# Start and end of a fused attention and gated-MLP block: how the modulation weight and c are read, which banks hold the first queries, and when the last output tiles are finished

## The chip, the cores and the metric

The kernel runs on one core of a Trainium2 chip. The metric is the device time of one execution in microseconds (us). The time before is the median of four runs, and one further execution was taken by the hardware profiler; all durations below come from that one.

## The reference

```python
mod = (silu(c) @ w_mod).reshape(1, 6, 1, 512)      # c: 1x512, w_mod: 512x3072
sa, ca, ga, sb, cb, gb = mod[:, 0..5]
h = layernorm(x) * (1 + ca) + sa                   # x: 1x2048x512
x = x + ga * A(h)      # 32 query heads over 8 cached key/value heads, 2048 keys, 128 wide, then wo
h = layernorm(x) * (1 + cb) + sb
x = x + gb * B(h)      # gelu(h @ w_in) halves z1, z2; layernorm(z2); w_sp @ z2 + b_sp; (z1 * g) @ w_out
```

All tensors are bf16. `A` is softmax attention without a mask: `q = h @ wq`, scores over the cached keys times 128^-0.5, softmax, times the cached values, then `@ wo`. In `B`, `w_sp` is 2048x2048 and mixes the rows.

## The kernel before, in words

The program is written out fully in Python; within each engine the order of instructions is the order of the source, laid out by hand (`manual_schedule`), with a table `at(unit, slot, ...)` that puts side work into slots of the attention loop. Semaphore waits follow from the tiles that an instruction reads and writes. PSUM has eight banks, held by three names: `misc` (two tiles of one bank), `o_ps` (two of one bank) and `s_ps` (two of two banks, by `bank2`). A name's tiles are taken in turn, so that a new tile waits for the one two before it.

**Start, before the attention loop.** ACT's queue reads c (`c_bf`, line 696) with element `4p + j` in partition p, column j. SP's queue reads the first tile of x, the first third of `w_mod` in four parts (`wmod_a`, L699; part kt holds rows `4p + kt`), half of the first keys (`k_nat`, L704), the query weight of the first key head (`wq_g`, L715), the second half of `k_nat`, more of x, and so on. DVE clears a tile `zeros`, and PE runs matmuls on it whose results nobody reads (`warm(n)`, L776). DVE and ACT make `silu(c)` in bf16 (`sc_bf`, L761 to L770). DVE and POOL normalise the first 128 rows of x (`xn1`, L691 to L680). PE makes shift and scale as columns from the four parts (`mod_part`, L868), with pairs of warm matmuls between, turns the normalised rows (L900), and DVE and ACT apply shift and scale while copying them out (`hT`, L828 and L908). Then PE turns four key blocks (`k_turn`, L883) which DVE and ACT copy (L886), 16 matmuls make the first 128 queries of four heads (L921) in the two banks of one `s_ps` tile, and DVE and ACT copy one bank each to `qT` (L929). One more warm matmul, and the loop begins.

**Attention loop.** 128 units of (key head, 128 query rows), eight slots each: PE makes scores (`qk`, L980), ACT takes the exponential (L987), PE multiplies with the values of the unit before (`pv`, L1002), DVE divides, and the output projection of an older unit runs beside it (L1034), as do the query projections (L947). The other two thirds of `w_mod` are read by POOL's queue in unit 2 (L1153) and used from unit 9 on (L792).

**MLP.** The spatial product is made in four chunks of 512 rows. In the last chunk the first 384 columns of each of the seven blocks of `yT` come first; the last 128 columns follow, block by block (L1347, with the bias added by a one-row matmul, L1355), and DVE multiplies them with `z1` (L1363). The output matmuls (L1368) trail by one block. `finish_tile` scales by `gb` (L1380), adds x (L1381) and issues the output DMA on ACT's queue (L1382). In the last chunk it is called for tiles 0, 1, 2 beside blocks f = 1, 3, 5:

```python
        if f % 2 == 1:
            finish_tile(last, f // 2, o2_last[f // 2])
```

**Fallback.** A flag says whether some softmax sum left a safe range; then `general_path` would redo everything. `redo = nc.values_load(flag...)` (L1418) loads it into a register of each of the five engines ahead of the last seven blocks, and `tc.If(redo != 0)` (L1432) is a compare-and-branch on each engine, which here jumps over the whole fallback to the end.

Of the kernel before, what the change touches and what calls it, by code (L numbers as in the profile page):

```python
# [10 lines left out]
BF16 = mybir.dt.bfloat16  # L11
FP32 = mybir.dt.float32
ACT = mybir.ActivationFunctionType
ALU = mybir.AluOpType
AX = mybir.AxisListType
P = 128
# [559 lines left out]
def kernel(  # L576
# [19 lines left out]
    nc = tc.nc  # L596
    _, S, D = A_x.shape
    _, HKV, SK, DH = A_k_cache.shape
    HQ = A_wq.shape[1] // DH
    REP = HQ // HKV  # L600
# [5 lines left out]
    NDT = D // P  # L606
# [3 lines left out]
    CT = 512 // P  # L610
# [8 lines left out]
    out_dram = out[0].rearrange("(t p) d -> p t d", p=P)  # L619
# [3 lines left out]
    HK = SK // 2  # L623
    k_rows = A_k_cache[0, 0, 0:HK].rearrange("(p t) d -> p t d", p=P)
    v_rows = A_v_cache[0, 0, 0:HK].rearrange("(p t) d -> p t d", p=P)
    wmod_dram = w_mod.rearrange("(p dt) n -> p dt n", p=P)
    c_dram = c[0].rearrange("(p j) -> p j", p=P)
    win_dram = B_w_in.rearrange("(dt p) f -> p dt f", p=P)
    wout_dram = B_w_out.rearrange("(ft p) d -> p ft d", p=P)

# [2 lines left out]
    flag = flagp.tile([1, 1], mybir.dt.int32, name="flag")  # L633
# [4 lines left out]
    res = fast.enter_context(tc.tile_pool(name="res", bufs=1))  # L638
# [4 lines left out]
    late = free_b.enter_context(tc.tile_pool(name="late", bufs=2, side="right"))  # L643
    early = free_a.enter_context(tc.tile_pool(name="early", bufs=2))

    x_sb = res.tile([P, NT, D], BF16, name="x_sb")
    ga_rows = res.tile([P, D], FP32, name="ga_rows")
    gb_rows = res.tile([P, D], FP32, name="gb_rows")
# [11 lines left out]
    ident = res.tile([P, P], BF16, name="ident")  # L660
    ones_bf = res.tile([P, P], BF16, name="ones_bf")

    def bank(name):
        return psum.tile([P, 512], FP32, name=name)

    def bank2():
        return psum.tile([P, 1024], FP32, name="s_ps")

    def rstd_of(mv, n, tag):

        ve = stat.tile([P, CT], FP32, name=f"ve_{tag}")
        nc.gpsimd.tensor_scalar(
            out=ve[:, :n], in0=mv[:, :, 1], scalar1=LN_EPS, scalar2=None, op0=ALU.add
        )
        rstd = stat.tile([P, CT], FP32, name=f"rstd_{tag}")
        nc.gpsimd.tensor_tensor(out=rstd[:, :n], in0=ve[:, :n], in1=mhalf[:, :n], op=ALU.pow)
        return rstd

    def normalise(dst, src, mv, rstd):
        nc.vector.tensor_scalar(  # L680
            out=dst,
            in0=src,
            scalar1=mv,
            scalar2=rstd,
            op0=ALU.subtract,
            op1=ALU.mult,
        )

    def ln_stats(mv, j, src):
        st = stat.tile([P, 1, nc.vector.BN_STATS_DIM], FP32, name="bnst")  # L690
        nc.vector.bn_stats(out=st[:, 0, :], in_=src)  # L691
        nc.vector.bn_aggr(out=mv[:, j, :], in_=st[:])


    c_bf = res.tile([P, NDT], BF16, name="c_bf")
    nc.scalar.dma_start(out=c_bf[:], in_=c_dram)
    nc.sync.dma_start(out=x_sb[:, 0, :], in_=x_dram[:, 0, :])
    for kt in range(NDT):
        nc.sync.dma_start(out=wmod_a[:, kt, :], in_=wmod_dram[:, kt, 0 : 2 * D])  # L699
# [53 lines left out]
        nc.sync.dma_start(out=x_sb[:, tiles, :], in_=x_dram[:, tiles, :])  # L753
    load_wo(0, nc.sync)


    zeros = late.tile([P, REP, DH], BF16, name="onorm", bufs=3)
    nc.vector.memset(zeros[:], 0.0)
    nc.vector.memset(ones_bf[:], 1.0)
    c_f = res.tile([P, NDT], FP32, name="c_f")  # L760
    nc.vector.tensor_copy(out=c_f[:], in_=c_bf[:])  # L761
    en = res.tile([P, NDT], FP32, name="en")
    nc.scalar.activation(out=en[:], in_=c_f[:], func=ACT.Exp, scale=-1.0)
    nc.vector.tensor_scalar_add(out=en[:], in0=en[:], scalar1=1.0)
    sig = res.tile([P, NDT], FP32, name="sig")
    nc.vector.reciprocal(out=sig[:], in_=en[:])
    sc = res.tile([P, NDT], FP32, name="sc")
    nc.vector.tensor_tensor(out=sc[:], in0=c_f[:], in1=sig[:], op=ALU.mult)
    sc_bf = res.tile([P, NDT], BF16, name="sc_bf")
    nc.vector.tensor_copy(out=sc_bf[:], in_=sc[:])  # L770

    def warm(n):

        w_ps = bank("o_ps")
        for k in range(n):
            nc.tensor.matmul(  # L776
                w_ps[:].rearrange("p (r d) -> p r d", r=REP),
                lhsT=zeros[:, 0, :],
                rhs=zeros[:],
                start=True,  # L780
                stop=True,
            )
# [26 lines left out]
    def ln1_stats(j0, n):  # L809
        for j in range(j0, j0 + n):  # L810
            ln_stats(mv1, j, x_sb[:, j, :])
        return rstd_of(mv1[:, j0 : j0 + n, :], n, "ln1")

    def ln1_norm(j0, n, rstd):
        xns = []
        for j in range(j0, j0 + n):
            xn = res.tile([P, D], BF16, name="xn1", bufs=4)
            normalise(xn[:], x_sb[:, j, :], mv1[:, j, 0:1], rstd[:, j - j0 : j - j0 + 1])
            xns.append(xn)
        return xns  # L820
# [65 lines left out]
            copy(out=kT0[:, part[0] * P : (part[-1] + 1) * P], in_=k_ps[:, 0 : n * P])  # L886


    xns0 = ln1_norm(0, 1, ln1_stats(0, 1))
    mc_ps = bank("misc")  # L890
    warm(10)
    for kt in range(NDT - 1):
        mod_part(kt, mc_ps)
        warm(2)
    x_ps = []
    for half in range(2):
        x_ps.append(bank(("misc", "o_ps")[half])[:].bitcast(BF16))
        for k in range(2):
            dt = 2 * half + k
            nc.tensor.transpose(  # L900
                x_ps[half][:, k * P : (k + 1) * P], xns0[0][:, dt * P : (dt + 1) * P], ident[:]
            )
# [3 lines left out]
    for k in range(2):  # L906
        ln1_mod(hTs[0][:, k, 0:P], x_ps[0][:, k * P : (k + 1) * P], k)
        nc.scalar.activation(  # L908
            out=hTs[0][:, 2 + k, 0:P],
            in_=x_ps[1][:, k * P : (k + 1) * P],  # L910
            func=ACT.Identity,
            scale=modc[:, NDT + 2 + k : NDT + 3 + k],
# [1 line left out]
        )  # L914
    k_turn((0, 1, 2, 3), (nc.vector.tensor_copy, nc.scalar.copy))
    qTs = {0: early.tile([P, REP, 512], BF16, name="qT")}
    q_ps = bank2()
    for n, dt in enumerate((0, 2, 1, 3)):
        for hh in range(REP):
            c0 = hh // 2 * 512 + hh % 2 * P  # L920
            nc.tensor.matmul(  # L921
                q_ps[:, c0 : c0 + P],
                lhsT=wqs[0][:, dt, hh * DH : (hh + 1) * DH],
                rhs=hTs[0][:, dt, 0:P],
                start=(n == 0 and hh % 2 == 0),
                stop=(n == NDT - 1 and hh % 2 == 1),
            )
    for hf, copy in enumerate((nc.vector.tensor_copy, nc.scalar.copy)):
        copy(  # L929
            out=qTs[0][:, 2 * hf : 2 * hf + 2, 0:P],  # L930
            in_=q_ps[:, hf * 512 : hf * 512 + 2 * P].rearrange("p (h q) -> p h q", h=2),
        )
    warm(1)

    def qproj(b, heads, c0, n):

# [376 lines left out]
    for f in range(NFT):  # L1313
# [6 lines left out]
        out=ok1[:], in0=rall[:], scalar1=1.0 / SAFE, scalar2=None, op0=ALU.is_ge  # L1320
# [8 lines left out]
        out=bad[:], in0=okm[:], scalar1=-1.0, scalar2=1.0, op0=ALU.mult, op1=ALU.add  # L1329
# [37 lines left out]
    def o2_mm(dst, yT, jj, f):  # L1367
        nc.tensor.matmul(  # L1368
            dst,
            lhsT=yT[:, f, jj * P : (jj + 1) * P],  # L1370
            rhs=wout_sb[:, f, :],
            start=(f == 0),
            stop=(f == NFT - 1),
        )

    def finish_tile(t, jj, src):
        j = t * CT + jj
        tmp = mlp.tile([P, D], FP32, name="tmp", bufs=2)
        yout = mlp.tile([P, D], BF16, name="yout", bufs=2)
        nc.vector.tensor_tensor(out=tmp[:], in0=src, in1=gb_rows[:], op=ALU.mult)  # L1380
        nc.vector.tensor_tensor(out=yout[:], in0=tmp[:], in1=x_sb[:, j, :], op=ALU.add)  # L1381
        nc.scalar.dma_start(out=out_dram[:, j, :], in_=yout[:])  # L1382

    yTs = {}

    def o2_tile(t, jj):
        o2 = bank("o_ps")
        for f in range(NFT):
            o2_mm(o2[:], yTs[t], jj, f)
        finish_tile(t, jj, o2[:])  # L1390

    last = NCH - 1
    n_a = 512 - P
# [15 lines left out]
    o2_last = [acc[jj // 2][:, (jj % 2) * 512 : (jj % 2 + 1) * 512] for jj in range(CT)]  # L1409
    yT = yTs[last]  # L1410
    for f in range(NFT):
        spatial(last, yT, f, 0, n_a)
        if f < CT:
            o2_tile(last - 1, f)
        if f > 0:
            for jj in range(CT - 1):
                o2_mm(o2_last[jj], yT, jj, f - 1)
    redo = nc.values_load(flag[0:1, 0:1], min_val=0, max_val=P)  # L1418
    for f in range(NFT):
        spatial(last, yT, f, n_a, P, bias_by_pe=True)  # L1420
        if f == 0:
            for jj in range(CT - 1):
                o2_mm(o2_last[jj], yT, jj, NFT - 1)
        else:
            o2_mm(o2_last[CT - 1], yT, CT - 1, f - 1)
        if f % 2 == 1:
            finish_tile(last, f // 2, o2_last[f // 2])
    o2_mm(o2_last[CT - 1], yT, CT - 1, NFT - 1)
    finish_tile(last, CT - 1, o2_last[CT - 1])
    fast.close()  # L1430

    with tc.If(redo != 0):  # L1432
        general_path(
            tc, A_x, A_k_cache, A_v_cache, A_wq, A_wo, B_x, B_w_in, B_w_sp, B_b_sp, B_w_out,
            c, w_mod, out,
        )
# [30 lines left out]
```

## Time and profile before

| what | value |
|---|---|
| median of 4 runs | 1324.24 us (1323.87 to 1324.52) |
| profiled execution: its time | 1324.25 us |
| profiled execution: span, first to last instruction | 1322.5 us |
| PE busy | 1312.0 us, 99% of the span |
| ACT busy | 1077.6 us, 81% |
| DVE busy | 472.6 us, 36% |
| mean granted TensorE clock | 0.999 |

How to read what follows. "PE" is TensorE's matmuls, "PEld" its weight loads, "DVE" VectorE, "ACT" ScalarE, "POOL" GpSimd, "SP" SyncE; a "q" after the name (SPq, ACTq) stands for the engine's instruction queue, with DMA issues, branches and semaphore waits, which are not counted as busy. A group's row gives the line of the source, the engine, the operation and the tiles (out<-in). A matmul's row is longer than its share of a stream: matmuls are pipelined. In the chain that ended last, each piece has its start, its length and what it was.

### The profile page before, as it was taken

How to read it: one execution, taken by the hardware profiler on the slowest of the kernel's cores; microseconds unless marked ns; L12 is line 12 of the kernel's file. 1: busy time of each engine (PE TensorE's matmuls, PEld its weight loads, DVE VectorE, ACT ScalarE, POOL GpSimd, SP SyncE). 2: the span in 40 equal slices, each digit the busy share in tenths (PEclk: the TensorE clock that was granted, in tenths of full speed). 3: DMA queues.
4: the chain of work that ended last, by engine and by line, in shares of the span. 5: the costliest groups of instructions: out<-in, count | busy, mean ns of one | idle time of the engine just before them, and what ended most of it. 6: DMA issues, size and time to landing. Idle time of an engine off the chain costs nothing.

```text
span 1322.5 us, 27873 instructions
## 1 busy us (share of the span) xinstructions
PE 1312.0 (99%) x12332; PEld 858.3 (65%) x12332; DVE 472.6 (36%) x1166; ACT 1077.6 (81%) x1061; POOL 48.9 (4%) x92
## 2 busy tenths in 40 slices
PE   8999999999999999999999999999999999999998
PEld 5666666666666666666666666666666666644445
DVE  5632222222222222222222222222222566794444
ACT  6898999999999999999999999999999999650000
POOL 1200000000000000000000000000000000020000
PEclk9999999999999999999999999999999999999999
DMA  6451022102111112111110221121101111144300
GB/s 179 128 117 33 13 49 37 37 13 53 25 29 33 34 37 37 29 37 37 33 33 17 53 37 30 21 53 18 34 16 21 25 32 31 33 112 84 69 21 26
DMA packets 148208, 58.12 MB, mean 44 GB/s; under 512 B 138384, under 2 KB 143760, under 8 KB 148080
## 3 DMA queue, kind: packets, MB, share of 16 engines
q1 hardware_dynamic: 141424, 37.78, 14.9%
q0 software_dynamic: 4208, 16.39, 4.2%
q10 hardware_dynamic: 2448, 2.10, 0.5%
q8 instruction: 98, 1.61, 0.5%
q14 instruction: 30, 0.25, 0.1%
HBM read 21.37 MB, written 2.10 MB: 18 GB/s over the span
## 4 chain that ended last, share of the span: by engine, by line
PE 99%; DMA 0%; DVE 0%; SPq 0%; issue 0%; ACT 0%
PE o_ps L1002 35%; PE s_ps L980 33%; PE misc L1034 8%; PE misc L947 8%; PE misc L1347 7%; PE s_ps L1193 2%; PE s_ps L1232 2%; PE o_ps L1368 1%; PE s_ps L1368 1%; DMA wq_g<-in_A_wq_dram 0%; PE misc L1104 0%; SPq L699 0%; DVE tmp L1380 0%; DVE yout L1381 0%; PE s_ps L921 0%; PE misc L1355 0%
## 5 line engine op out<-in xcount | busy, mean ns | idle before, releaser
L987 ACT ACTIVATE pT<-s_ps 128x1024 bf16<-128x1024 f32 x1024 | 1044.3, 1025 | 83.0 <-PE s_ps L980 8.9
L1002 PEld LDWEIGHTS <-pT 128*128 128x128 bf16 x8192 | 548.5, 98 | 241.2
L1002 PE MATMUL o_ps<-v,pT 128*128 128x129 bf16 x8192 | 631.4, 220 | 0.0
L980 PE MATMUL s_ps<-qT,kT 128*128 128x512 bf16 x2048 | 609.0, 379 | 0.7 <-ACT qT L929 0.7
L1013 DVE RECIPROCAL rall<-o_ps 128x2 f32<-128x2 f32 x256 | 43.7, 171 | 744.6 <-PE o_ps L1002 744.4
L980 PEld LDWEIGHTS <-kT 128*128 128x128 bf16 x2048 | 199.4, 98 | 119.2 <-issue 1.4
L1034 PE MATMUL misc<-wo_g,oT 128*128 128x512 bf16 x512 | 194.0, 379 | 0.0
L947 PE MATMUL misc<-hT,wq_g 128*128 128x512 bf16 (+2 forms) x528 | 189.6, 371 | 0.0
L1014 DVE TENSOR_TENSOR onorm<-o_ps,rall 128x256 bf16<-128x256 f32 x256 | 108.6, 424 | 9.0 <-DVE rall L1013 0.3
L1347 PE MATMUL misc<-wsp,z 128*128 128x512 bf16 (+2 forms) x560 | 100.7, 336 | 0.0
L958 DVE CAST qT<-misc 128x512 bf16<-128x512 f32 x127 | 86.2, 680 | 2.3 <-PE misc L947 2.2
L1347 PEld LDWEIGHTS <-z 128*128 128x128 bf16 x560 | 50.6, 98 | 48.5
L1047 DVE TENSOR_TENSOR xacc<-misc,xacc 128x512 f32<-128x512 f32 x112 | 76.1, 680 | 0.0
L947 PEld LDWEIGHTS <-wq_g 128*128 128x128 bf16 x528 | 50.6, 98 | 1.1 <-issue 0.2
L1034 PEld LDWEIGHTS <-oT 128*128 128x128 bf16 x512 | 50.1, 98 | 0.8
L1362 DVE TENSOR_TENSOR gb<-misc,bsp_bc 128x512 bf16<-128x512 f32 (+1 forms) x28 | 18.4, 658 | 59.1 <-PE misc L1347 59.1
L1193 PE MATMUL s_ps<-win_sb,hT 128*128 128x448 bf16 x128 | 27.0, 352 | 0.0
L1203 ACT ACTIVATE z<-s_ps 128x896 bf16<-128x896 f32 x16 | 14.7, 917 | 14.9 <-PE s_ps L1193 14.9
L1232 PE MATMUL s_ps<-hT,win_sb 128*128 128x512 bf16 x112 | 24.5, 379 | 0.0
L1240 ACT ACTIVATE z1T<-s_ps 128x1024 bf16<-128x1024 f32 x14 | 14.3, 1024 | 10.1 <-PE s_ps L1232 9.1
L691 DVE BATCH_NORM_STATS2 bnst<-x_sb 128x6 f32<-128x512 bf16 x32 | 21.9, 683 | 0.5
L715 POOL DMA_DIRECT2D wq_g<-in_A_wq_dram x7 | 5.3, 752 | 420.9 <-PE misc L947 420.9
(86 smaller groups left out, 281.6 us busy)
## 6 DMA issues: line engine op xcount, KB each, us to landing
wq_g<-in_A_wq_dram POOLq DMA_DIRECT2D x7, 512.0 KB, 3.9
v<-in_A_v_cache_dram POOLq DMA_DIRECT2D x7, 512.0 KB, 6.6
wo_g<-in_A_wo_dram POOLq DMA_DIRECT2D x7, 512.0 KB, 4.7
oT<-onorm SPq DMA_TRANSPOSE x128, 2.4
wsp<-in_w_mod_dram POOLq DMA_DIRECT2D x1, 2048.0 KB, 10.5
out_dram<-yout ACTq DMA_DIRECT2D x16, 128.0 KB, 1.7
win_sb<-in_B_w_in_dram POOLq DMA_DIRECT2D x1, 1792.0 KB, 7.7
x_sb<-in_A_x_dram SPq DMA_DIRECT2D x3, 512.0 KB, 5.6
```

What stands on the lines that cost most here:

```text
L947: nc.tensor.matmul(ps[0][:, o0 : o0 + n], lhsT=wqs[g][:, dt, hh * DH : (hh + 1) * DH], rhs=hTs[ch][:, dt, c0 : c0 + n], start=(dt == 0), s ...
L958: nc.vector.tensor_copy(out=dst, in_=src)
L980: nc.tensor.matmul(s_ps[:, h * 512 : (h + 1) * 512].rearrange("p (r q) -> p r q", r=REP), lhsT=groups[g]["kT"][:, kt * P : (kt + 1) * P], ...
L987: nc.scalar.activation(out=pTs[u][:, 2 * i : 2 * i + 2, :], in_=s_ps[:].rearrange("p (k q) -> p k q", k=2), func=ACT.Exp, scale=inv_sqrt_dh,)
L1002: nc.tensor.matmul(o_ps[:, hh % 2, 0 : DH + 1], lhsT=pTs[u][:, kt, hh * P : (hh + 1) * P], rhs=groups[g]["v1"][:, kt, 0 : DH + 1], start=( ...
L1013: nc.vector.reciprocal(out=rall[:, c0 : c0 + 2], in_=o_ps[:, :, DH])
L1014: nc.vector.tensor_tensor(out=onorms[u][:, hh - 1 : hh + 1, :], in0=o_ps[:, :, 0:DH], in1=rall[:, c0 : c0 + 2].unsqueeze(2).to_broadcast([ ...
L1034: nc.tensor.matmul(X_ps[:], lhsT=oTs[u][:, hh, :], rhs=groups[g]["wo"][:, hh, :], start=(hh == 0), stop=(hh == REP - 1),)
L1047: nc.vector.tensor_tensor(out=xaccs[j][:], in0=X_ps[:], in1=xaccs[j][:], op=ALU.add)
L1193: nc.tensor.matmul(ps[0][:, hf * 512 : hf * 512 + FC], lhsT=h2Ts[j // CT][:, dt, (j % CT) * P : (j % CT + 1) * P], rhs=win_sb[:, dt, FH + ...
L1232: nc.tensor.matmul(ps[0][:, k * 512 : (k + 1) * 512], lhsT=win_sb[:, dt, f * P : (f + 1) * P], rhs=h2Ts[2 * ch2 + k][:, dt, :], start=(dt ...
L1347: nc.tensor.matmul(g_ps[:, :n], lhsT=z2[:, st, f * P : (f + 1) * P], rhs=wsp[t][:, st, c0 : c0 + n], start=(st == 0), stop=(st == NT - 1 a ...
```

## The change

The change has four parts:

1. `w_mod` is read so that part dt holds the neighbouring rows `128 dt + p` (in place of `4p + kt`), for both reads of it. c, accordingly, is needed as element `128 j + p`.
2. c is read as four rows of 128 elements into a piece of a tile of the name `onorm`; PE turns it with the identity matrix after four of the warm matmuls, and DVE reads the turned c from a `misc` bank. The chain to `sc_bf` moves behind that in the source; six warm matmuls follow it.
3. The second half of the turned x goes to an `s_ps` tile in place of an `o_ps` one. The first queries go to two `misc` tiles of one bank each in place of one `s_ps` tile. Four warm matmuls come before the query matmuls, and two in place of one after them.
4. In the last chunk, tiles 0, 1, 2 are finished beside f = 1, 2, 3. The last tile is finished in two halves of 256 columns, the first written by ACT's queue, the second by SP's. The flag is loaded after all of that.

```diff
-    wmod_dram = w_mod.rearrange("(p dt) n -> p dt n", p=P)
-    c_dram = c[0].rearrange("(p j) -> p j", p=P)
+    wmod_dram = w_mod.rearrange("(dt p) n -> p dt n", p=P)
+    c_dram = c[0].rearrange("(j p) -> j p", p=P)
...
-    c_bf = res.tile([P, NDT], BF16, name="c_bf")
-    nc.scalar.dma_start(out=c_bf[:], in_=c_dram)
+    c_bf = late.tile([P, REP, DH], BF16, name="onorm", bufs=3)[0:NDT, 0, :]
+    nc.scalar.dma_start(out=c_bf, in_=c_dram)
...
+    warm(4)
+    c_ps = bank("misc")[:].bitcast(BF16)
+    nc.tensor.transpose(c_ps[:, 0:NDT], c_bf, ident[0:NDT, 0:NDT])
+
     c_f = res.tile([P, NDT], FP32, name="c_f")
-    nc.vector.tensor_copy(out=c_f[:], in_=c_bf[:])
+    nc.vector.tensor_copy(out=c_f[:], in_=c_ps[:, 0:NDT])
...
     xns0 = ln1_norm(0, 1, ln1_stats(0, 1))
     mc_ps = bank("misc")
-    warm(10)
+    warm(6)
...
-        x_ps.append(bank(("misc", "o_ps")[half])[:].bitcast(BF16))
+        x_ps.append((bank("misc")[:] if half == 0 else bank2()[:, 0:512]).bitcast(BF16))
...
-    q_ps = bank2()
+    warm(4)
+    q_ps = [bank("misc"), bank("misc")]
     for n, dt in enumerate((0, 2, 1, 3)):
         for hh in range(REP):
-            c0 = hh // 2 * 512 + hh % 2 * P
             nc.tensor.matmul(
-                q_ps[:, c0 : c0 + P],
+                q_ps[hh // 2][:, hh % 2 * P : (hh % 2 + 1) * P],
...
-            in_=q_ps[:, hf * 512 : hf * 512 + 2 * P].rearrange("p (h q) -> p h q", h=2),
+            in_=q_ps[hf][:, 0 : 2 * P].rearrange("p (h q) -> p h q", h=2),
         )
-    warm(1)
+    warm(2)
...
-    def finish_tile(t, jj, src):
+    def finish_tile(t, jj, src, parts=1):
...
-        nc.vector.tensor_tensor(out=tmp[:], in0=src, in1=gb_rows[:], op=ALU.mult)
-        nc.vector.tensor_tensor(out=yout[:], in0=tmp[:], in1=x_sb[:, j, :], op=ALU.add)
-        nc.scalar.dma_start(out=out_dram[:, j, :], in_=yout[:])
+        w = D // parts
+        for k in range(parts):
+            s = slice(k * w, (k + 1) * w)
+            nc.vector.tensor_tensor(out=tmp[:, s], in0=src[:, s], in1=gb_rows[:, s], op=ALU.mult)
+            nc.vector.tensor_tensor(out=yout[:, s], in0=tmp[:, s], in1=x_sb[:, j, s], op=ALU.add)
+            (nc.scalar, nc.sync)[k].dma_start(out=out_dram[:, j, s], in_=yout[:, s])
...
-    redo = nc.values_load(flag[0:1, 0:1], min_val=0, max_val=P)
     for f in range(NFT):
         spatial(last, yT, f, n_a, P, bias_by_pe=True)
...
-        if f % 2 == 1:
-            finish_tile(last, f // 2, o2_last[f // 2])
+        if 1 <= f < CT:
+            finish_tile(last, f - 1, o2_last[f - 1])
     o2_mm(o2_last[CT - 1], yT, CT - 1, NFT - 1)
-    finish_tile(last, CT - 1, o2_last[CT - 1])
+    finish_tile(last, CT - 1, o2_last[CT - 1], parts=2)
     fast.close()
 
+    redo = nc.values_load(flag[0:1, 0:1], min_val=0, max_val=P)
     with tc.If(redo != 0):
```

More of the change, by code (lines that the diff above doesn't have):

```diff
@@ L759 @@
     nc.vector.memset(ones_bf[:], 1.0)
-    c_f = res.tile([P, NDT], FP32, name="c_f")
-    nc.vector.tensor_copy(out=c_f[:], in_=c_bf[:])
[L762 to L770, printed above, removed]
     def warm(n):
@@ L886, in k_turn @@
             copy(out=kT0[:, part[0] * P : (part[-1] + 1) * P], in_=k_ps[:, 0 : n * P])
+    warm(4)
+    c_ps = bank("misc")[:].bitcast(BF16)
+    nc.tensor.transpose(c_ps[:, 0:NDT], c_bf, ident[0:NDT, 0:NDT])
+    c_f = res.tile([P, NDT], FP32, name="c_f")
+    nc.vector.tensor_copy(out=c_f[:], in_=c_ps[:, 0:NDT])
+    en = res.tile([P, NDT], FP32, name="en")
+    nc.scalar.activation(out=en[:], in_=c_f[:], func=ACT.Exp, scale=-1.0)
+    nc.vector.tensor_scalar_add(out=en[:], in0=en[:], scalar1=1.0)
+    sig = res.tile([P, NDT], FP32, name="sig")
+    nc.vector.reciprocal(out=sig[:], in_=en[:])
+    sc = res.tile([P, NDT], FP32, name="sc")
+    nc.vector.tensor_tensor(out=sc[:], in0=c_f[:], in1=sig[:], op=ALU.mult)
+    sc_bf = res.tile([P, NDT], BF16, name="sc_bf")
+    nc.vector.tensor_copy(out=sc_bf[:], in_=sc[:])
     xns0 = ln1_norm(0, 1, ln1_stats(0, 1))
     mc_ps = bank("misc")
-    warm(10)
+    warm(6)
     for kt in range(NDT - 1):
@@ L1389, in o2_tile @@
             o2_mm(o2[:], yTs[t], jj, f)
-        finish_tile(t, jj, o2[:])
+        finish_tile(t, jj, o2)
     last = NCH - 1
```

## The prediction

> **What bounds the kernel now.** I read the page first. Of the chain that ended last, PE is 99% of the span: from about 20 us to 1316 us PE is full (10.00 busy of 10.00 in the windows 20 to 30 and 1306 to 1316), and the built program of the changed kernel has the same instructions in the same order between those two points on every engine. So only the first 12 us, where PE waits, and the last 8 us, after PE has ended, can change. For the first I read the chain in order of time (start, length, what), where the third number after a name is the line.
>
> ```profile
> 3.56 6.21 DMA wq_g<-in_A_wq_dram
> ...
> 10.92 0.44 DVE qT L929
> ...
> 11.38 0.38 ACT qT L929
> ...
> 11.80 0.59 PE s_ps L980 x2
> ```
>
> The query weight lands at 9.8, 16 matmuls (L921) take 1.08, and then DVE and ACT copy the two halves of the queries one after the other. The waits of the first 24 us say why (sum, times, longest):
>
> ```profile
> ACT qT L929 <- DVE qT L929: 1.6, 1, 1.6
> ...
> PE o_ps L883 <- ACT hT L908: 0.5, 1, 0.5
> ```
>
> ACT's copy waits for DVE's, though they read different banks of one tile. At the end I read the chain once more:
>
> ```profile
> 1315.58 0.69 DVE yout L1381
> 1316.28 0.21 DVE yT L1363
> 1316.48 0.05 issue
> 1316.53 0.40 PE s_ps L1368
> ```
>
> The last column of yT waits for the third output tile on DVE. L1363 starts 0.27 after L1355's matmul wherever DVE is free (1311.52 to 1311.79, 1314.27 to 1314.53); here it is 1315.64 to 1316.19. Then L1380 at 1316.96 and L1381 at 1317.68, 0.69 each, and the last DMA issue at 1318.41. What lies between that and 1322.5 is not the DMA alone. The rows of the branch around the fallback (duration, first to last start):
>
> ```profile
> L1432 SPq COMPARE_BRANCH  x1: 53/53/53, 1242.8 to 1242.8; - x1
> L1432 PEldq COMPARE_BRANCH  x1: 4027/4027/4027, 1316.5 to 1316.5; - x1
> L1432 DVEq COMPARE_BRANCH  x1: 72/72/72, 1317.7 to 1317.7; - x1
> L1432 ACTq COMPARE_BRANCH  x1: 54/54/54, 1318.8 to 1318.8; - x1
> L1432 DVEq EVENT_SEMAPHORE  x1: 21/21/21, 1320.6 to 1320.6; - x1
> ...
> L1432 ACTq EVENT_SEMAPHORE  x1: 17/17/17, 1321.5 to 1321.5; - x1
> ```
>
> DVE and ACT come out of the branch 2.8 and 2.7 us after it, PE after 4.0. In the DMA rows an 8 KB instruction packet starts 0.9 to 1.1 after each of DVE's and ACT's branches: the engine fetches the code it jumped to. The last DMA has landed at 1320.3 (SP's wait on it ends there); ACT, at 1321.5, ends the kernel, and a barrier of 1.0 follows. SP branched at 1242.8, where nobody waits, and the DMA rows of 1243 to 1247 show the same mark, one packet 0.9 after its branch and the next 2.3 later (forty slices of 0.1; queue, packets, MB, share):
>
> ```profile
> DMA  0000000200000000000000000000002000000000
> ...
> q14 instruction: 2, 0.02, 1.2%
> ```
>
> **The change, part by part.** All sums are against the profiled execution: span 1322.5, and 1324.25 with the 1.75 around it. The median of the runs, 1324.24, is the same number.
>
> *c by PE.* c arrived at 2.81 (c_f, L761). Now four rows are read in place of 128 short ones and PE turns them after four warm matmuls. These run 0.43 apart from 1.18, so PE is free at 2.9; the turn needs c, which I put at 2.8 at the latest, by the row of before; fewer pieces can make it earlier and that gains nothing. A PE result reaches DVE 0.27 later (L1355 to L1363), so c_f is at about 3.25 and sc_bf ends at 4.5 in place of 4.04. DVE's first statistics (L691, 3.95) and with them POOL's two steps and xn (L680, 5.87 to 6.28) are queued behind it and move by the same 0.45, to 6.7. Nobody is late: the six other warm matmuls end at 5.2 in place of 5.1, the third part of the modulation matmuls waits for its DMA until 6.65 (PEld idle 0.78), and xn is turned at 7.3. Cost 0; without that DMA wait it would be about 0.1, PE's own delay.
>
> The Trainium skill, "TensorE: Matmul & The Clock Gate", Part 1, speaks against breaking the warm row. In this trace the warm matmuls' weight loads come at 0.43 until 4.14 and at 0.37 and 0.22 after it, some 3.3 us after the first. The page says that the full clock needs a window of about 3.4 us of sustained work, free-running, so by the rule a hole in the row may cost a second slow window. By the rows there is no hole, c being there at 2.8 and PE free at 2.9, and the cost is 0.
>
> The bound from rows alone, if PE should stay slow until the modulation matmuls are done: ten of the warm matmuls at 0.43 in place of 0.216, 2.1, less the idle 0.78: 1.3. I take 0 and keep 1.3 as a small case.
>
> *Weight layout.* Four reads of 256 KB in the same place of SP's queue, 2 KB pieces as before, but 6 KB apart in place of 24 KB. No row shows what the distance is worth. Bounds: the DMA rows of 2 to 6 us move 242 to 338 GB/s, 16% to either side of their mean, and 1 MB takes 3.6 us at that mean: 0.55 earlier or later. Of earlier, PE's own row (warm matmuls, then modulation, then the key turns) lets only about 0.2 through. I take 0 and keep -0.2 and +0.55. The 2 MB read of the rest on POOL's queue lands 10.5 us after its issue in unit 2 and is first used at 95.7 (L792): 0 either way.
>
> *Key turns and the four warm matmuls before the queries.* The second turn no longer waits for ACT (0.5 above), but nothing on the path gains from it: wq_g lands at 9.8 anyway. The four warm matmuls wait for DVE's key copy (L886, 8.68 to 8.96), then take four times 0.216 (1.51 for seven, L1368 in the chain of time): PE reaches the queries at 9.87 in place of 9.81. Cost 0.06. If the keys land later, all of the 0.86 is in the open.
>
> *Separate banks.* In the built program ACT's copy waits for PE and no longer for DVE. The matmuls end at 10.95, DVE's copy runs 10.98 to 11.41 and ACT's (0.37) beside it. Two warm matmuls, 0.43, end at 11.38, beneath DVE's copy. The first score matmul starts at 11.45 in place of 11.80. Its successors in the chain up to 20 us are PE, DVE's key copy, statistics and xn, each released by that matmul, so the gain stays. Sum of the start: -0.35.
>
> *Finishing order.* Tiles 0, 1, 2 are finished one step after another (f = 1, 2, 3); DVE is then 0.3 late for two of the yT columns, but PE asks for those a step later (1313.05 and 1314.43 against 1312.4 and 1313.95). The last yT is free at 1315.91: PE ends 0.28 earlier, last matmul at 1316.25. Then halves: 128x256 between the rows 0.29 (128x128) and 0.69 (512), and 0.425 for L929: 0.42. Four of them with the gaps of before (0.03 where one needs the other, overlapping by 0.08 where not): 1316.68, 17.13, 17.47, 17.92, end 1318.34. Against 1318.37 the halving has eaten the 0.28: -0.03.
>
> *The last half's DMA on SP, and the flag's load after it.* ACT issues the first half at 1317.6, loads the flag (473 ns at L1418, hidden at 1297.6 before), branches at 1318.5 and is out at 1321.2. DVE: load 0.54, branch near 1318.5, out at 1321.3. PE: 0.49 later, less the 0.28: 1320.8. POOL and SP load it where they did, in the built order. But SP now issues at 1318.38 (0.34, as ACT's), branches at 1318.8 and pays its jump in the open: out at 1321.5, by ACT's 2.67. Only then do its waits run, 8 for the DMA lanes (five took 1320.3 to 1320.6, 0.07 each: 0.57) and 12 for the barrier (1320.6 to 1321.3, 0.06 each: 0.7): 1322.75 against the 1321.5 at which ACT released SP. The tail costs +1.25. Bounds: -0.2 if SP's jump is free (then DVE's 1321.3 is last), and +2.9 if the fetches stand in line (below).
>
> Sum: 1324.25 - 0.35 + 1.25 = 1325.15. What this kernel's measurement can tell from no change is about 0.2%, 2.65 us, so this is "the same".
>
> **Rivals.** (1) SP's jump costs nothing in the open. For: POOL's branch at 1242.5 was out at 1242.7. Against: the two packets after SP's. Then -0.35 - 0.2: 1323.7. (2) The start gives nothing: the weight lands later, or the warm matmuls stand in the way. For: the layout has no row, and the 0.86 of warm matmuls has only 0.8 of cover. Start 0 to +0.5, tail as forecast: 1325.5 to 1326.0. The forms in which a part doesn't do what it says (copies still in turn, no faster reads) end here too. (3) Slower: the fetches queue. Before, the branches lay 1.2 and 1.0 apart; now ACT's, DVE's and SP's lie within 0.35. For: PE asked 1.2 before DVE and both came out at 1320.6. If each waits for the fetch before by the 0.95 that parted DVE and ACT, SP, third of the three, is out 1.6 later (1321.2, 1322.15, 1323.1 for 1321.5): 1326.75. If each waits a whole 2.7, it is 5.1 later: 1330.25. It is slower by more than 2.65 from an extra 1.75 on.
>
> **How the numbers follow.** The forecast, alone within 1324.7 to 1325.7, 0.56; rival 1 0.16; rival 2 0.13; rival 3 0.10, of which 0.07 beyond the 0.2%; the slow clock after all, 1326.45, 0.03, of which 0.01 beyond it. For faster by over 0.2% I find no term: -0.2 and -0.55 at the best do not reach it, and 0.02 is left for what I don't see. So 0.02 faster, 0.08 slower, 0.9 within. The range takes in rival 1 with the layout's -0.2, 1323.5, and the mild form of rival 3, 1326.8.
>
> **What would show it.** Right: ACT's query copy beside DVE's and the first score matmul at 11.4 to 11.5; L1363's last column at 0.27 after L1357; SP's branch near 1318.5 (0.35 earlier on the new clock) and its first wait after it 2.7 later, with SP last in the barrier. Wrong: query matmuls past 10.2; SP's first wait at the landing of its own DMA; any difference between 20 and 1306 us.

## The result and the profile after

| what | before | after |
|---|---|---|
| median of the runs set against each other | 1324.21 us (1323.46 to 1325.02, 60 runs) | 1325.73 us (1324.90 to 1326.34, 40 runs) |
| profiled execution: its time | 1324.25 us | 1325.82 us |
| profiled execution: span | 1322.5 us | 1324.0 us |

The ratio is 1.0011, 95% interval 1.0007 to 1.0016: 1.52 us longer, by medians, where 0.91 was forecast (1325.15). It lies within the predicted range and within the 0.2% that were called "the same", but it is a real loss, and it lies just past the 1325.7 up to which the forecast itself reached, in the band of the second rival (1325.5 to 1326.0).

The start, first. The chain in order of time of the changed kernel (start, length, what; the warm matmuls are L763 here, the queries L923, the first scores L982):

```profile
8.43 0.16 DVE modc L790
...
9.29 0.21 DVE kT L873
9.50 0.04 issue
9.54 1.02 PE o_ps L763 x4
10.57 0.89 PE misc L923 x16
11.46 0.43 PE o_ps L763 x2
11.89 0.03 issue
11.92 0.59 PE s_ps L982 x2
```

and two of its waits (sum, times, longest):

```profile
ACT qT L931 <- PE misc L923: 1.7, 1, 1.7
...
PE o_ps L763 <- DVE kT L873: 0.9, 1, 0.9
```

ACT's query copy now waits for PE and not for DVE, as forecast. But the query matmuls begin at 10.40 by the timeline (the chain counts them from 10.57, where the warm ones end), past the 10.2 that the prediction named as a sign of error. The four warm matmuls, from 9.54 on, stand in the open ahead of them: the query weight, the cover that the prediction gave them, had landed at 8.9 (5.3 after its issue, 6.2 before), and DVE's key copy that releases them began at 9.21 (the chain counts only its last 0.21, from 9.29) instead of 8.68. The queries end 0.58 later than before (11.46 against 10.88), and the two copies side by side give 0.46 of it back: the first score matmul starts at 11.92, 0.12 later than before and not 0.35 earlier.

The end. The rows of the branch around the fallback (duration in ns, first to last start), here L1437:

```profile
L1437 SPq EVENT_SEMAPHORE  x8: 17/17/17, 1321.8 to 1322.3; - x8
...
L1437 ACTq COMPARE_BRANCH  x1: 54/54/54, 1318.6 to 1318.6; - x1
L1437 DVEq COMPARE_BRANCH  x1: 72/72/72, 1318.7 to 1318.7; - x1
L1437 SPq COMPARE_BRANCH  x1: 53/53/53, 1318.9 to 1318.9; - x1
...
L1437 ACTq EVENT_SEMAPHORE  x1: 17/17/17, 1321.2 to 1321.2; - x1
L1437 DVEq EVENT_SEMAPHORE  x1: 21/21/21, 1321.6 to 1321.6; - x1
```

SP, which branched at 1242.8 before, now branches at 1318.9, comes out at 1321.8, runs its eight waits until 1322.3, and only then the barrier's. That is the order forecast. Taking off the 0.12 that the start put on everything, the steps stand at: last matmul 1316.25 (forecast 1316.25), end of the second half on DVE 1318.37 (1318.34), SP's branch 1318.8 (1318.8), SP out 1321.7 (1321.5). So the end costs 1.45 in this trace (the time is 1.57 longer, less 0.12) where 1.25 was forecast, and the start 0.12 where -0.35 was.

### The profile page after: what moved, and what is told of

It reads as the page before. It is cut to its first block, busy times and chain, and to the rows that moved or that the text cites. A ratio compares the mean times of both kernels' runs of the same rounds, so it can differ in the third digit from the quotient of the medians.

```text
span 1324.0 us, 27890 instructions
## 1 busy us (share of the span) xinstructions
PE 1313.6 (99%) x12338; PEld 859.0 (65%) x12338; DVE 472.8 (36%) x1168; ACT 1077.5 (81%) x1061; POOL 48.9 (4%) x92
## 4 chain that ended last, share of the span: by engine, by line
PE 99%; DVE 0%; issue 0%
PE o_ps L1004 35%; PE s_ps L982 33%; PE misc L1036 8%; PE misc L949 8%; PE misc L1349 7%; PE s_ps L1195 2%; PE s_ps L1234 2%; PE o_ps L1370 1%; PE o_ps L763 1%; PE s_ps L1370 1%; PE misc L1106 0%; PE misc L1357 0%; PE misc L833 0%; PE misc L923 0%; DVE yout L1386 0%; DVE tmp L1385 0%
## 5 line engine op out<-in xcount | busy, mean ns | idle before, releaser
L982 PE MATMUL s_ps<-qT,kT 128*128 128x512 bf16 x2048 | 609.0, 379 | 0.0
L982 PEld LDWEIGHTS <-kT 128*128 128x128 bf16 x2048 | 199.3, 98 | 118.7 <-DVE qT L931 0.5
```

What stands on the lines that cost most here:

```text
L982: nc.tensor.matmul(s_ps[:, h * 512 : (h + 1) * 512].rearrange("p (r q) -> p r q", r=REP), lhsT=groups[g]["kT"][:, kt * P : (kt + 1) * P], ...
```

## The experiments

Ten kernels, each timed in 9 to 11 runs beside the kernel before on the same chip. The intervals of single ratios are about 0.0009 to either side, 1.2 us, as large as most of the steps. So a median by itself settles only the large ones; for the others the trace of the run has to show the same step. Differences below are of medians, against the kernel before in the same call (1324.10, 1324.21 and 1324.18 in the three calls).

**Halves of the change: the start alone, the end alone.** The first takes the changed file up to `finish_tile` and the old one after it, the second the reverse.

> The start of the change, with the end of the kernel before (tiles at f = 1, 3, 5, whole last tile on ACT's queue, flag loaded early). Theory T (the loss sits in SP's jump at the end; the start is about even): against before +0.1 us, between -0.4 and +0.5, and the end of its trace as before: ACT last out of the branch. Rival R (the start lost its clock window and its four extra warm matmuls, and carries half or more of the loss): +0.7 us or more. Clock: if the turn of c breaks the warm row, PE's warm matmuls stay at 0.43 until about 6.2 us as in the changed kernel; if that was chance, they may be fast from 4.5.

> The start of before, with the end of the change. T: +1.4 us against before (1.2 to 1.6), SP's first wait after its branch 2.7 to 2.9 later and SP last in the barrier; the warm matmuls fast from about 4.5. R: +0.7 or less.

Start alone: 1324.23, ratio 1.0000 (0.9991 to 1.0009), +0.13. End alone: 1325.60, ratio 1.0013 (1.0004 to 1.0022), +1.50; its fastest run (1325.28) is slower than the slowest of the kernel before (1324.85). The sum, 1.63, answers for the 1.52. The whole loss is in the last 8 us, and the start, which was to give 0.35, gives nothing.

**The flag loaded before the last seven blocks again, everything else as changed.**

```diff
+    redo = nc.values_load(flag[0:1, 0:1], min_val=0, max_val=P)
     for f in range(NFT):
...
-    redo = nc.values_load(flag[0:1, 0:1], min_val=0, max_val=P)
     with tc.If(redo != 0):
```

> The change, with the flag loaded where before loads it (ahead of the last seven blocks); the second half of the last tile stays on SP's queue. T: SP's jump alone sets the end, so no more than 0.1 us is gained against the changed kernel (+1.4 to +1.6 against before), though ACT and DVE branch 0.5 earlier. Rival F (the late load of the flag on ACT, DVE and PE is what costs): 0.5 less than the changed kernel, +1.0 against before. Rival Q (the four code fetches get in each other's way): SP's jump gets shorter than the 2.9 of the changed kernel once the other branches lie further ahead, by as much as 0.2.

1325.42, ratio 1.0010 (1.0001 to 1.0019), +1.32. ACT and DVE branch 0.7 and 0.8 earlier than in the changed kernel (1318.0, 1317.9) and come out at 1320.6 and 1321.0; nobody gains much, because SP still branches at 1318.8:

```profile
L1437 SPq EVENT_SEMAPHORE  x8: 17/17/17, 1321.4 to 1322.0; - x8
...
L1437 SPq COMPARE_BRANCH  x1: 53/53/53, 1318.8 to 1318.8; - x1
```

It is out at 1321.4, 2.6 later in place of 2.9. So the place of the load is not the cause: with the early load 0.2 of the 1.5 is gone by medians. Whether the shorter jump means that the code fetches hinder each other, the mild side of the prediction's third rival, is not shown: in two later traces where the three branches lie as close together as in the changed kernel (without the four warm matmuls, and with c turned late), SP's jump took 2.76 and 2.74. In the DMA rows of the changed kernel the three 8 KB packets start 0.9 to 1.0 after the three branches (1319.58, 1319.76, 1319.96) and run partly beside each other, so no fetch waited for a whole other one.

**Both halves of the last tile written by ACT's queue.** SP then has no late DMA and branches early, as before.

```diff
-            (nc.scalar, nc.sync)[k].dma_start(out=out_dram[:, j, s], in_=yout[:, s])
+            nc.scalar.dma_start(out=out_dram[:, j, s], in_=yout[:, s])
```

> The change, with both halves of the last tile on ACT's queue; the flag is still loaded late. T: SP branches near 1243 again and its jump is hidden; ACT becomes last: issue at 1318.5, 0.34, load 0.47, branch at 1319.4, out at 1322.1, then SP's last barrier wait and 1.0: 0.9 less than the changed kernel, +0.6 against before. Rival F: no gain against the changed kernel, since the load stays late.

1325.18, ratio 1.0008 (0.9999 to 1.0017), +1.08. Less than the changed kernel, but by 0.44 (each against its own before) and not by the 0.9 expected. Its branch rows and its DMA issues:

```profile
L1437 SPq COMPARE_BRANCH  x1: 53/53/53, 1242.6 to 1242.6; - x1
...
L1437 ACTq COMPARE_BRANCH  x1: 54/54/54, 1319.6 to 1319.6; - x1
...
L1437 ACTq EVENT_SEMAPHORE  x1: 17/17/17, 1322.3 to 1322.3; - x1
```

```profile
L1387 ACTq DMA_DIRECT2D out_dram<-yout x17: 338/339/825, 1229.0 to 1318.2; - x17
```

SP's jump is hidden at 1242.6, and the last engine out is ACT. Its issue of the second half took 0.825 in place of 0.34 (the row's longest against its median), so that its load and its branch came at 1319.1 and 1319.6. These 0.49 make up the difference from what was expected. No run has both halves on ACT's queue and the flag loaded early, so what the halving by itself costs there is not shown.

**Without the four warm matmuls before the queries**, everything else as changed.

```diff
-    warm(4)
     q_ps = [bank("misc"), bank("misc")]
```

> The change without the four warm matmuls ahead of the query matmuls; all else is left. Theory W: since the weight lands at 8.9 to 9.2 here, these four (1.02 us from 9.54 on in the changed kernel, behind DVE's key copy) are what the queries wait for; without them the queries start once ACT's second half of hT is there, near 9.4 to 9.7, and the whole is 0.7 to 0.9 us shorter than the changed kernel, +0.6 to +0.8 against before. Rival K (they keep the clock or cover a wait that takes their place): less than 0.3 us shorter.

1324.99, ratio 1.0005 (0.9996 to 1.0014), +0.78: 0.74 less than the changed kernel, and this although its trace has a late query weight (10.03, 6.5 after the issue). Its chain:

```profile
3.55 6.47 DMA wq_g<-in_A_wq_dram
10.03 0.05 issue
10.07 1.08 PE misc L922 x16
...
11.60 0.59 PE s_ps L981 x2
```

The queries start when the weight lands, and the first score matmul at 11.60, 0.32 earlier than in the changed kernel. Four warm matmuls, which were costed at 0.06, cost 0.74 by medians. In the changed kernel's own trace they hold the queries back by 0.83: the last thing that these need otherwise, ACT's second half of hT, was there at 9.57, and they begin at 10.40.

**The separate banks alone, on the kernel before.**

```diff
-        x_ps.append(bank(("misc", "o_ps")[half])[:].bitcast(BF16))
+        x_ps.append((bank("misc")[:] if half == 0 else bank2()[:, 0:512]).bitcast(BF16))
...
-    q_ps = bank2()
+    q_ps = [bank("misc"), bank("misc")]
```

> The kernel before, with only the banks changed: the second half of the turned x in s_ps, the queries in two tiles of one bank; no extra warm matmuls. My step: ACT's copy runs beside DVE's, the first score matmul is 0.40 to 0.45 earlier than in before (two copies of 0.42 and 0.37 side by side), -0.4 us. Rival: something else ends last there (keys, DVE's statistics) and less than 0.2 comes through. By H the clock is full at 4.4 to 4.6 (unbroken row).

1323.72, ratio 0.9996 (0.9987 to 1.0005), -0.49. Its chain in order of time:

```profile
9.37 0.21 DVE kT L886
9.58 0.04 issue
9.62 1.08 PE misc L920 x16
10.70 0.02 issue
10.72 0.38 ACT qT L928
11.10 0.04 issue
11.14 0.59 PE s_ps L979 x2
```

With a key copy as late as in the changed kernel (9.37, there 9.29) but no warm matmuls behind it, the queries start at 9.62 and the first scores at 11.14, 0.78 earlier than in the changed kernel. From the end of the query matmuls to the first scores it takes 0.46, in the kernel before 0.92; this holds in every trace here, 0.46 with separate banks (0.57 where PE ran at half speed) and 0.92 without. The gain that the prediction wrote down for the banks is real.

**The row order of `w_mod` alone, on the kernel before.** Only `wmod_dram` is changed; c keeps its old order, so the modulation is computed from mismatched rows.

> The kernel before, with only the row order of the modulation weight changed; c keeps its old order, so the modulation values are wrong and the time alone counts. If the nearer rows are what makes the query weight land 0.6 us earlier (5.3 to 5.6 after its issue in the changed starts, 5.9 to 6.2 in the old ones): 5.3 to 5.6 here, queries at 9.0 to 9.4, -0.3 to -0.6 us against before. Rival C (it is the 128 short pieces of c that are gone): 5.9 to 6.2 and no change. By H the clock is full at 4.4 to 4.6 (unbroken row).

1324.24, ratio 0.9999 (0.9990 to 1.0008), +0.03. No gain from reads 6 KB apart in place of 24 KB is seen, which is the value that was taken, though the interval leaves room for 1 us either way. The query weight landed late rather than early in its trace, 6.4 after its issue.

**c turned after ten warm matmuls instead of after four**, to see what a late c does to PE's clock.

```diff
-    warm(4)
+    warm(10)
     c_ps = bank("misc")[:].bitcast(BF16)
...
-    warm(6)
```

> The change with the turn of c behind all ten warm matmuls of the start in place of behind four, so that the row of warm matmuls is not broken. Theory H (the turn in the middle of the row costs PE its clock window): the pitch falls from 0.43 to 0.22 at 4.4 to 4.6 us, as in the kernel before, and not at 5.5 to 6.4 as in the four traces with the broken row. Rival P (chance): 5.5 or later here too. The time: silu(c) is ready 1.5 to 2 us later (c_f at about 5.3), which the earlier clock only half repays: the first score matmul at 12.0 to 12.6, 0.2 to 0.8 us longer than the changed kernel; by P 1.0 or more.

1327.52, ratio 1.0029 (1.0019 to 1.0039), +3.31: 1.8 longer than the changed kernel, more than either theory gave. PE waits 1.31 for `sc_bf`, and then the granted clock falls. Windows of its start (length, busy time of PE, PEld, DVE, ACT and POOL, then the granted clock, DMA share and GB/s):

```profile
7.50:8.10 0.60, 0.60 (x15) 0.36 (x13) 0.00 (x0) 0.00 (x0) 0.52 (x2) 1.00 1.09 365
...
8.20:14.90 6.70, 5.78 (x42) 3.68 (x40) 2.04 (x8) 1.44 (x4) 0.20 (x1) 0.50 1.26 239
...
15.00:15.20 0.20, 0.20 (x2) 0.10 (x1) 0.20 (x1) 0.00 (x0) 0.00 (x0) 1.00 1.10 358
```

From 8.13 to 14.96 PE ran at half speed, and the first scores came at 15.0. Its slowest and fastest runs lie 4.3 apart, so not every execution need have had this.

**The finishing order alone, on the kernel before**, and **the order with the separate banks**. The order's edit:

```diff
-        if f % 2 == 1:
-            finish_tile(last, f // 2, o2_last[f // 2])
+        if 1 <= f < CT:
+            finish_tile(last, f - 1, o2_last[f - 1])
```

> The kernel before with tiles 0, 1, 2 finished beside f = 1, 2, 3 in place of 1, 3, 5 alone. By the prediction's step: the last yT starts 0.27 after L1355's matmul, the last matmul and with it the last tile, ACT's DMA issue and ACT's branch move 0.28 earlier, so the time is 0.25 to 0.3 less than before. Rival: DVE, asked for tiles in three consecutive steps, makes an earlier yT late that PE asks for at once, and PE ends where it did: 0 difference, with idle time of PE before L1368 in steps 1 to 3.

> The kernel before with two things alone: separate banks for the first queries and for the second half of the turned x, and tiles 0, 1, 2 finished beside f = 1, 2, 3; the last tile is finished whole and written by ACT's queue, the flag loaded before the last seven blocks as before. If the two gains add up (0.49 measured for the banks alone, 0.28 from the chain of before for the order): 0.6 to 0.9 less than the kernel before, 1323.35 to 1323.65, score matmul about 0.3 to 0.9 after the query copies start, last matmul 0.33 after the last yT that follows its matmul by 0.27, and ACT's branch, then its semaphore, last before the barrier, SP's branch far ahead. If the order gives nothing because PE's end was set elsewhere: 0.4 to 0.5 less.

Order alone: 1323.86, ratio 0.9998 (0.9989 to 1.0007), -0.32. The last column of yT in its timeline (start, length, engine, line, operation, tiles, shape, and in brackets the idle time before it):

```profile
1315.53 0.23 PE L1355 MATMUL misc<-bsp_bc,ones_bf 1*128 1x128 bf16 x1
...
1315.79 0.29 DVE L1363 TENSOR_TENSOR yT<-misc,z1T 128x128 bf16<-128x128 f32 x1 [1.08 <-PE misc L1355]
```

DVE is idle when the column comes, and takes it 0.26 after the matmul (0.55 before, 1315.64 to 1316.19).

Order and banks together: 1323.34, ratio 0.9994 (0.9985 to 1.0003), -0.84; the two alone add up to -0.81. Its slowest run (1324.08) is faster than the fastest of the changed kernel (1324.90), and its median is 2.4 below it. Against the kernel before the runs overlap and the interval includes 1, so that this gain rests on both steps being seen in the trace. Its chain, at the queries and at the last column of yT:

```profile
9.71 1.08 PE misc L920 x16
...
11.24 0.59 PE s_ps L979 x2
...
1315.16 0.17 PE misc L1354
1315.34 0.02 issue
1315.36 0.30 DVE yT L1362
```

From the end of the queries (10.78) to the first scores it takes 0.46, and the column follows its matmul (L1354) at once; before, the third output tile (L1381) stood between. The branches:

```profile
L1431 SPq COMPARE_BRANCH  x1: 53/53/53, 1242.3 to 1242.3; - x1
...
L1431 ACTq COMPARE_BRANCH  x1: 54/54/54, 1318.0 to 1318.0; - x1
...
L1431 ACTq EVENT_SEMAPHORE  x1: 17/17/17, 1320.4 to 1320.4; - x1
```

SP stays early, and ACT is out at 1320.4 in place of 1321.5. SP no longer waits for it: the longest wait in SP's barrier is 0.03, where it was 0.21 before. The last transfer landed at 1319.4, and SP's remaining waits follow it without a gap, so in this version its landing sets the end. The median is below those of both kernels.

## Why the prediction was right, and where it was not

**The end: right in its mechanism, 0.2 to 0.25 too small.** The prediction put the loss on SP's branch being moved from 1242.8 to behind its own late DMA, with its jump of 2.67 and its waits in the open. The trace shows each of these steps within 0.05 up to the branch. Counted from the branch's end, as the prediction's 2.67 was, SP's jump took 2.80 (3.00 with the end alone, 2.56 to 2.71 in three other runs), and its twenty waits took 1.36 where 1.27 was summed. Both terms were a little short; why the jump varies is open. The end alone measured +1.50, the trace +1.45. The first rival, a free jump for SP (1323.7), is refuted; so is the hard form of the third, where whole fetches wait for each other: three engines that branched within 0.3 came out within 0.6.

**The start: the step that failed is "Cost 0.06" for the four warm matmuls.** The prediction let them run in the shadow of the query weight's landing at 9.8, and added that all of the 0.86 is in the open "if the keys land later". The keys did not land later, but both edges of the shadow moved. The weight landed at 8.9, and DVE's key copy came 0.53 later, because PE's chain up to `modc` ended 0.53 later: the full clock came at 6.40 in place of 4.44. The 0.8 of cover was luck of the one trace that was read: it is there in two of the twelve traces (before, and the end alone), while in the other ten the weight landed between 1.2 before and 0.2 after the end of DVE's key copy. A late clock is not the only reason: with the layout alone the clock came at 4.35, but the modulation weight's third part landed at 7.5, and the key copy ended at 9.86. Taking the four away gave back 0.74. With that in place of 0.06 the prediction's sum for the start is -0.35 + 0.68 = +0.33; measured were +0.13 by medians and +0.12 in the trace. This is the second rival (0.13 of the chance), whose "for" was just this: 0.86 of warm matmuls and 0.8 of cover.

**Separate banks: right.** -0.41 in the prediction's sum (the -0.35 without the 0.06), -0.46 between the end of the queries and the first scores in the traces, and -0.49 by medians for the banks alone.

**c by PE and the layout: taken as 0, and no cost seen.** The layout alone measured +0.03. c's turn was not run alone. PE turned c at 3.00 with no hole in the row (forecast 2.9), and the changed kernel without the four warm matmuls stands 0.72 below the end alone (+0.78 against +1.50), more than the banks' 0.49 give, so the medians leave no room for a cost of c's turn; with the width of their intervals they do not exclude one.

**The slow clock: not the turn's doing, as far as these runs tell.** The weight loads of the warm row in the kernel before and in the one with the finishing order alone, whose starts are the same code (start, length):

```profile
4.14 0.15 PEld L776 LDWEIGHTS <-onorm 128*128 128x128 bf16 x1 [0.28 <-issue]
4.51 0.10 PEld L776 LDWEIGHTS <-onorm 128*128 128x128 bf16 x1 [0.22 <-issue]
```

```profile
4.14 0.15 PEld L776 LDWEIGHTS <-onorm 128*128 128x128 bf16 x1 [0.28 <-issue]
4.57 0.15 PEld L776 LDWEIGHTS <-onorm 128*128 128x128 bf16 x1 [0.28 <-issue]
...
6.72 0.12 PEld L776 LDWEIGHTS <-onorm 128*128 128x128 bf16 x2
6.96 0.46 PEld L868 LDWEIGHTS <-wmod_a 128*128 128x128 bf16 x8
```

In the first the pitch shortens after 4.14; in the second it is 0.43 until 6.5. With the unbroken row the full clock came at 4.35 to 4.72 in four traces and at 6.74 to 7.01 in three; with c's turn in it, at 5.55 to 7.3 in five. So an onset as late as in the changed kernel needs no break: theory H, which expected 4.4 to 4.6 wherever the row is unbroken, fits c turned late (4.72) and the layout alone (4.35) and fails for the banks alone (6.97). All twelve lie within 2.95 of each other. Whether the break shifts the odds can't be told from twelve traces. Nor was a late onset dear by itself: with the order alone, the first scores came at 11.68 in spite of it.

**The finishing order and the halving: right.** -0.28 forecast and -0.32 by medians for the order, whose last matmul came 0.27 earlier in the trace without the 0.12 by which its start was ahead; the halving ate it: without the start's 0.12 DVE's last step ended at 1318.37 in the changed kernel, exactly where 1317.68 + 0.69 had it before. The halves bought no earlier issue of the last transfer, and brought SP's queue into the end.

**Open.** Why the query weight landed 5.3 to 5.6 after its issue in four runs of the changed start, but 6.1 and 6.5 in two others with the same DMAs, and 5.8 to 6.4 with the old start, the layout alone among them. Three of the four are from one chip and the two from another; the fourth's chip is not known. On the first chip the old start took 5.8 to 6.1, on the second 6.0 and 6.4. The layout and c's fewer pieces are thus neither shown nor excluded as a cause.

## What to carry to other kernels

Before a queue is given the last transfer, look at what that engine does after it: here SP had its far jump, eight waits and the barrier's behind it, and 1.5 us were added to the end for a transfer that was not issued earlier. Work that is hidden only by the landing of one DMA in one trace is not hidden: price it as if the landing came at the early end and its own release at the late end. A change whose parts pull both ways is worth splitting: the banks and the order gain 0.8 us here, four warm matmuls lose 0.7, and the new end, which has the order's 0.3 in it, loses 1.5.

## What the runs showed of the hardware

- The branch over the fallback, whose target lies far away, took 2.4 to 3.2 us on ACT, DVE and SP until the engine's next instruction, and 3.4 to 4.0 on PE; POOL's took 0.2, and why it is so much shorter is not shown. The Trainium skill, "Runtime: NRT & Kernel Launch", section "Instruction fetch mechanics", says that a taken branch out of the fetched window has to wait for a DMA fetch of its target; it gives no duration, and the 2.4 to 4.0 are these runs' answer. The 8 KB instruction packets that start 0.9 to 1.0 after the branches of the changed kernel agree with it.
- PE's clock fell back in the middle of its work in two traces, at 8.13 for 6.83 us (c turned late) and at 11.36 for 3.41 us (the end alone), with the granted clock at 0.50. The longest idle stretch of PE's matmuls before it was 1.31 in the one and 0.78 in the other; the kernel before, with stretches of up to 0.98, did not fall, nor did the layout alone, with 1.23, 1.09 and 0.99. In "TensorE: Matmul & The Clock Gate", Part 1, the Trainium skill gives a free-running window of about 3.4 us, and an idle window as what sends the clock back. The lengths, one and two times 3.41, agree with the window; but no run here had PE idle for a whole one, so shorter gaps were enough, in some traces and not in others. What decides is open.
- Three traces whose starts are the same code reached the full clock at 4.44, at 4.53 and, in the third, only at 6.74 us.
